# A pair's sigmoid moved behind the next step's copy, and the squares, scaling and moves of x spread over one more step each

## The chip, the cores and the metric

One core of one Trainium2 chip. The metric is device time in microseconds (us): the median of three runs of the kernel before is 1411.33 us (1408.41 to 1411.77). All times of single instructions come from one profiled execution of 1410.37 us, whose span from first to last instruction is 1408.6 us.

## The reference

Two stages. The first is attention over channels, for two matrices of 6016 x 256; the second is a gated two-layer network on 12032 rows of 256.

```
qn = q / (norm(q, axis=1) + 1e-06);  kn = k / (norm(k, axis=1) + 1e-06)
s  = kn.T @ qn / tau;  a = softmax(s, -1)          # 256 x 256
x  = (v @ a).reshape(12032, 256)
xn = x / sqrt(mean(x * x, -1) + 1e-06) * rms_g
g  = xn @ w_gate;  val = xn @ w_val                # 256 -> 1536
out = (g * sigmoid(g) * val) @ w_out               # 1536 -> 256
```

## The kernel before

The first part reads q and k and forms the score matrices (that of the second matrix beside block 0). The rows of v are worked on in 24 blocks of 512 rows (12 of each matrix, the last of each 384 rows). A block j is 12 steps f = 0 to 11, one for each 128 of the 1536 hidden columns, and in the same steps the next block's x is made ready, so that TensorE (PE) always has hidden columns to work on. Every engine takes its instructions in the order in which the code issues them; that order is written by hand, in the loop over `steps` at lines 909 to 922: the step itself, then the output products of an earlier step, then what the table `ready` lists for this f (for block j + 1), then what `extra` lists.

There are two kinds of steps. Steps 0, 1, 8 and 9 are plain (`emit_hidden`, L603): six products of 512 columns for the gate (pg), six for the value (pv). ScalarE (ACT) takes the sigmoid of pg (L624), VectorE (DVE) multiplies (L627, L634). Steps 2 to 7, 10 and 11 come in pairs (`emit_pair`, L543), two hidden blocks together by a scheme with fewer products: the even step of a pair is its gate step (k = 0), the odd one its value step (k = 1). Each has 21 products of 256 columns in four groups, each group in a PSUM bank of its own: (1,), (2, 6), (5, 7), (3, 4). ACT copies the first group out (L575, "the copy"); then DVE adds the others up in four instructions (L580 to L583). After the gate step's four sums ACT takes the sigmoid of the gate (L587), GpSimd (POOL) multiplies it by the gate (L588), and after the value step's sums POOL multiplies by the value, in two halves (L595). The halves are then rounded on ACT (L534, gh) in the next step, and DVE takes the remainder (L540, gl). The output products (L654, po) follow three steps later.

PSUM has four banks for the steps (tag "gv"). A pair step takes all four, a plain step two, in turn: the second group of a step can start when the bank of four tiles before is free, which is when L580 of the step before has read it. So a late L580 stops PE one step later, at the second group of a pair step or at pv of a plain step; a late L627 of step 9 stops PE at the third group of step 10.

The next block's x: step 0 moves v (L359), step 1 splits it (L341, L342). Steps 2 and 3 end with the products of x, one half (two tiles of 128 rows) each (`emit_x`, L377, px, 12 matmuls). ACT squares them with a running sum (L388), POOL makes the factor 1/rms (L397, L401, rr), ACT scales (L413, xn). Two transposes on DVE (L449, xw) and 16 DMAs issued one after the other by SyncE (SP, L456, xnT) turn x. In step 8 ACT scales by g (L471) and DVE forms four differences (L477, xp); steps 9 and 10 split the eight operands ("round 0" and "round 1", L487 on ACT and L489 on DVE).

In block 1 the pairs' weights are built (`build_s`, from odd steps), and in block 10 the softmax of the second matrix runs in steps 5 to 9.

Of the kernel before, what the change touches and what calls it, by code (L numbers as in the profile page):

```python
# [8 lines left out]
F32 = mybir.dt.float32  # L9
F32R = mybir.dt.float32r  # L10
U32 = mybir.dt.uint32
AF = mybir.ActivationFunctionType
# [7 lines left out]
def kernel(  # L20
# [312 lines left out]
    def half_tiles(j, h):  # L333
        return list(range(2 * h, min(2 * h + 2, blocks[j][2])))
# [33 lines left out]
    def emit_x(j, h):  # L368
        ah, al = a_hl[blocks[j][0]]
        vh, vl = vT[j]  # L370
        ts = half_tiles(j, h)
        psum, tag = (ps_s, "s") if j >= WINO and h else (ps_m, "m") if j else (ps_gv, "gv")
        px = psum.tile([P, 2, C], F32, tag=tag, name=f"px_{j}_{h}")
        for c in range(KC):
            for i, t in enumerate(ts):
                for m, (w, x) in enumerate(((vh, ah), (vl, ah), (vh, al))):
                    nc.tensor.matmul(  # L377
                        out=px[:, i, :], lhsT=w[:, c, t * P:(t + 1) * P], rhs=x[:, c, :],
                        start=(i == 0 and c == 0 and m == 0),
                        stop=(c == KC - 1 and m == 2),  # L380
                        skip_group_check=True,
                    )
        if h == 0:
            xnt[j] = xn_p.tile([P, BT, C], F32, tag="xn", name=f"xn_{j}")
        xn = xnt[j][:, 2 * h:2 * h + 2, :]
        ss = st_p.tile([P, 2], F32, tag="ss", name=f"ss_{j}_{h}")
        for i in range(len(ts)):
            nc.scalar.activation(  # L388
                out=xn[:, i, :], in_=px[:, i, :], func=AF.Square, scale=C ** -0.5,
                accum_out=ss[:, i:i + 1],  # L390
            )
        xps[j, h] = (px, ss)

    def emit_rr(j, h):
        px, ss = xps[j, h]
        nn = len(half_tiles(j, h))
        nc.gpsimd.tensor_scalar(  # L397
            out=ss[:, :nn], in0=ss[:, :nn], scalar1=1e-6, scalar2=None, op0=ALU.add
        )
        rr = st_p.tile([P, 2], F32, tag="rr", name=f"rr_{j}_{h}")  # L400
        nc.gpsimd.tensor_tensor(out=rr[:, :nn], in0=ss[:, :nn], in1=mhalf[:, :nn], op=ALU.pow)  # L401
        xps[j, h] = (px, rr)
# [140 lines left out]
    def emit_pair(j, f):  # L543
# [31 lines left out]
        nc.scalar.activation(out=zz[:, 3:4], in_=ps[0], func=AF.Copy)  # L575
        n = nt * P
        if k:
            th, zg = zs.pop((j, p))
        run_rounds()
        nc.vector.tensor_tensor(out=zz[:, 0:5:4], in0=ps[1], in1=twice(zz[:, 3:4]), op=ALU.add)  # L580
        nc.vector.tensor_tensor(out=zz[:, 1:3], in0=ps[2], in1=twice(zz[:, 4:5]), op=ALU.add)  # L581
# [1 line left out]
        nc.vector.tensor_tensor(out=zz[:, 1:3], in0=ps[3], in1=zz[:, 1:3], op=ALU.add)  # L583
        run_subs()
        if k == 0:
            th = pool["z"].tile([P, 2 * BN], F32, tag="th", name=f"th_{j}_{p}", bufs=1)
            nc.scalar.activation(out=th[:, :2 * n], in_=z[:, :2 * n], func=AF.Sigmoid)  # L587
            nc.gpsimd.tensor_tensor(out=th[:, :2 * n], in0=th[:, :2 * n], in1=z[:, :2 * n], op=ALU.mult)  # L588
            zs[j, p] = (th, z)
            return  # L590
        for i in range(2):
            hh = zg[:, i * n:(i + 1) * n]
# [86 lines left out]
    with tc.manual_schedule():  # L679
# [102 lines left out]
        decode_w(0)  # L782
        for h in range(2):
            emit_x(0, h)
        emit_rr(0, 0)
        emit_rr(0, 1)
        load_w(2)
# [88 lines left out]
            for c in range(KC):  # L876
                split_v(n, c, nc.vector if n > 1 else nc.gpsimd)

        def x_part(h):
            def go(n):  # L880
                emit_x(n, h)
                emit_rr(n, h)
            return go

        def xn_part(h):
            return lambda n: emit_xn(n, h)

        ready = {
            0: (v_moves,),
            1: (v_splits,),  # L890
            2: (x_part(0),),
            3: (x_part(1), xn_part(0)),
            4: (xn_part(1), emit_xT_move),
            8: (emit_xT_parts,),
            9: (lambda n: emit_xT_round(n, 0),),
            10: (lambda n: emit_xT_round(n, 1),),
# [1 line left out]
        ready0 = {  # L898
            1: (v_moves,),
            2: (v_splits,),  # L900
            4: (x_part(0),),
            5: (xn_part(0),),
            6: (x_part(1),),
            7: (xn_part(1),),
            8: (lambda n: emit_xT_first(n, 0),),
            9: (lambda n: emit_xT_first(n, 1),),
        }
# [52 lines left out]
```

## Time and profile before

| what | us |
|---|---|
| median of 3 runs | 1411.33 (1408.41 to 1411.77) |
| the profiled execution | 1410.37 |
| its span | 1408.6 |
| PE busy | 1332.9 (95%) |
| DVE busy | 1064.1 (76%) |
| POOL busy | 671.8 (48%) |
| ACT busy | 636.1 (45%) |

A matmul of 256 columns is shown with some 280 ns, but one starts every 0.12 us: the records overlap, so PE's share says little and its starts and idle times say more. "[0.50 <-DVE z L580]" behind a row is the engine's idle time before it and what ended it. A row of a timeline merges like instructions ("x2"), and its length is from the first's start to the last's end.

### The profile page before, as it was taken

The page shows a single profiled execution, that of the slowest core. Times are in us where ns is not written, and L with a number is a line of the kernel's source. Part 1 is how long each engine was busy: PE and PEld are TensorE (multiplying, and loading weights), DVE is VectorE, ACT ScalarE, POOL GpSimd, SP SyncE. Part 2 cuts the span into 40 slices and gives each one's busy share as a digit, 9 for nine tenths or more (in the row PEclk, how much of TensorE's full clock was granted, in tenths as well). Part 3 has the DMA queues.
Part 4 walks back from the last instruction along what each step waited for, and adds up shares of the span by engine and source line. Part 5 has one row for each costly group of instructions (what it writes and reads, how often), then busy time and mean ns, then how long its engine had stood idle before and what let it go on. Part 6 is the DMA issues. An engine that isn't in the chain of part 4 may idle for free.

```text
span 1408.6 us, 24669 instructions
## 1 busy us (share of the span) xinstructions
PE 1332.9 (95%) x9420; PEld 1243.4 (88%) x9420; DVE 1064.1 (76%) x1597; ACT 636.1 (45%) x1244; POOL 671.8 (48%) x500
## 2 busy tenths in 40 slices
PE   8877979899999999999989999999999999999998
PEld 7766868799999999999979999999999999999998
DVE  4588847787787787787776787787787787787775
ACT  4445634444444444444444444444444444444442
POOL 1045623445545455455534445455455455545544
PEclk9989989999999999999999999999999999999999
DMA  9666310101111111111102111111111111111000
GB/s 305 210 186 200 115 30 16 31 20 42 31 24 39 32 25 36 34 25 31 36 7 46 28 24 36 33 25 35 34 26 33 34 28 31 34 24 31 22 22 12
DMA packets 150871, 71.61 MB, mean 51 GB/s; under 512 B 109281, under 2 KB 136929, under 8 KB 150753
## 3 DMA queue, kind: packets, MB, share of 16 engines
q1 hardware_dynamic: 150752, 70.04, 20.0%
q8 instruction: 74, 1.21, 0.4%
q14 instruction: 45, 0.36, 0.1%
HBM read 46.40 MB, written 12.32 MB: 42 GB/s over the span
## 4 chain that ended last, share of the span: by engine, by line
PE 48%; DVE 23%; ACT 9%; issue 8%; SPq 5%; DMA 4%; POOL 2%; DVEq 0%; ACTq 0%; POOLq 0%
PE p L563 14%; PE po L654 13%; PE pv L613 6%; PE s L175 5%; SPq L456 5%; PE px L377 5%; PE pg L613 4%; DVE z L580 4%; DVE z L581 3%; DVE xt L489 3%; ACT th L587 3%; DVE z L583 3%; POOL z L595 2%; DVE z L582 2%; DMA xnT<-xw 2%
## 5 line engine op out<-in xcount | busy, mean ns | idle before, releaser
L654 PE MATMUL po<-w,gh 128*128 128x256 f32 x2256 | 410.2, 280 | 1.2 <-ACT gh L534 1.2
L654 PEld LDWEIGHTS po<-w,gh 128*128 128x128 f32 x2256 | 353.0, 189 | 10.9 <-ACT gh L534 1.8
L563 PE MATMUL p<-xt,w 128*128 128x256 f32 (+1 forms) x2112 | 315.1, 283 | 13.4 <-DVE z L580 9.2
L654 PE MATMUL po<-w,gl 128*128 128x256 f32 x1128 | 316.1, 280 | 1.8 <-DVE gl L540 1.8
L588 POOL TENSOR_TENSOR th<-th,z 128x1024 f32<-128x1024 f32 (+1 forms) x88 | 206.7, 2349 | 214.5 <-ACT th L587 214.5
L595 POOL TENSOR_TENSOR z<-th,z 128x512 f32<-128x512 f32 (+1 forms) x176 | 219.7, 1269 | 164.7 <-DVE z L583 164.7
L563 PEld LDWEIGHTS p<-xt,w 128*128 128x128 f32 x2112 | 276.9, 189 | 18.9 <-DVE z L580 13.3
L534 ACT ACTIVATE gh<-z 128x512 fp32r<-128x512 f32 (+1 forms) x264 | 163.9, 622 | 228.4 <-POOL z L595 214.1
L563 PE MATMUL p<-xt,s 128*128 128x256 f32 (+1 forms) x1584 | 217.9, 282 | 2.2 <-DVE z L582 1.1
L654 PEld LDWEIGHTS po<-w,gl 128*128 128x128 f32 x1128 | 212.7, 189 | 2.7 <-DVE gl L540 2.7
L540 POOL TENSOR_TENSOR gl<-z,gh 128x512 fp32r<-128x512 f32 (+1 forms) x88 | 120.9, 1374 | 174.5 <-ACT gh L534 173.0
L563 PEld LDWEIGHTS p<-xt,s 128*128 128x128 f32 x1584 | 199.9, 189 | 3.7 <-PE p L563 2.1
L580 DVE TENSOR_TENSOR z<-p,z 128x512 f32<-128x512 f32 (+1 forms) x176 | 118.0, 670 | 103.5 <-ACT z L575 98.9
L613 PE MATMUL pv<-xt,w 128*128 128x512 f32 (+1 forms) x672 | 175.6, 397 | 14.4 <-DVE z L580 14.4
L613 PE MATMUL pg<-xt,w 128*128 128x512 f32 (+1 forms) x672 | 177.8, 400 | 3.1 <-DVE th L627 2.0
L587 ACT ACTIVATE th<-z 128x1024 f32<-128x1024 f32 (+1 forms) x88 | 91.3, 1037 | 174.3 <-DVE z L583 174.3
L613 PEld LDWEIGHTS pv<-xt,w 128*128 128x128 f32 x672 | 125.1, 189 | 50.4 <-DVE z L580 23.3
L540 DVE TENSOR_TENSOR gl<-z,gh 128x512 fp32r<-128x512 f32 (+1 forms) x176 | 133.1, 769 | 31.2 <-ACT gh L534 24.6
L613 PEld LDWEIGHTS pg<-xt,w 128*128 128x128 f32 x672 | 120.2, 190 | 25.2 <-DVE th L627 3.2
L583 DVE TENSOR_TENSOR z<-p,z 128x512 f32<-128x512 f32 (+1 forms) x176 | 119.6, 680 | 19.4 <-DVE z L582 1.4
L581 DVE TENSOR_TENSOR z<-p,z 128x512 f32<-128x512 f32 (+1 forms) x176 | 119.6, 680 | 19.4 <-DVE z L580 1.4
L175 PE MATMUL s<-raw 128*128 128x256 f32 x376 | 93.1, 408 | 24.9 <-DMA raw<-in_k_dram 24.9
(94 smaller groups left out, 1423.3 us busy)
## 6 DMA issues: line engine op xcount, KB each, us to landing
v<-in_v_dram SPq DMA_DIRECT2D x88, 128.0 KB, 3.7
out_dram<-ob SPq DMA_DIRECT2D x88, 128.0 KB, 2.2
xnT<-xw SPq DMA_DIRECT2D x320, 32.0 KB, 1.9
raw<-in_q_dram SPq DMA_DIRECT2D x27, 256.0 KB, 4.4
raw<-in_k_dram SPq DMA_DIRECT2D x27, 256.0 KB, 4.6
raw<-in_q_dram SPq DMA_DIRECT2D x9, 512.0 KB, 5.7
raw<-in_k_dram SPq DMA_DIRECT2D x9, 512.0 KB, 6.7
wraw<-in_moe_w_gate_dram SPq DMA_DIRECT2D x12, 256.0 KB, 2.9
```

The costliest lines, as they stand in the source:

```text
L175: nc.tensor.matmul(out=s_ps[b][:, c, :], lhsT=r[:, 1, t, c * P:(c + 1) * P], rhs=r[:, 0, t, :], start=(t0 + t == 0 and c == 0), stop=(t0 + ...
L534: nc.scalar.activation(out=gh, in_=hh, func=AF.Copy)
L540: engine.tensor_tensor(out=gl, in0=hh, in1=f32(gh), op=ALU.subtract)
L563: nc.tensor.matmul(out=t[:, i, :h], lhsT=wm[wi], rhs=xm[xi], start=(i == 0 and q == 0), stop=(q == 2), skip_group_check=True,)
L580: nc.vector.tensor_tensor(out=zz[:, 0:5:4], in0=ps[1], in1=twice(zz[:, 3:4]), op=ALU.add)
L581: nc.vector.tensor_tensor(out=zz[:, 1:3], in0=ps[2], in1=twice(zz[:, 4:5]), op=ALU.add)
L583: nc.vector.tensor_tensor(out=zz[:, 1:3], in0=ps[3], in1=zz[:, 1:3], op=ALU.add)
L587: nc.scalar.activation(out=th[:, :2 * n], in_=z[:, :2 * n], func=AF.Sigmoid)
L588: nc.gpsimd.tensor_tensor(out=th[:, :2 * n], in0=th[:, :2 * n], in1=z[:, :2 * n], op=ALU.mult)
L595: nc.gpsimd.tensor_tensor(out=o, in0=i0, in1=i1, op=ALU.mult)
L613: nc.tensor.matmul(out=t[:, :n], lhsT=wgv[wi][:, f, c, wj, :], rhs=x[xi][:, c, :n], start=(m == 0), stop=(m == 3 * KC - 1),)
L654: nc.tensor.matmul(out=o_ps[j][t // 2][:, t % 2, :], lhsT=g[:, t * P:(t + 1) * P], rhs=wo[w][:, f, :], start=(f == 0 and t % 2 == 0 and m ...
```

## The change

The sigmoid of a pair's gate and POOL's product with the gate are issued in the value step, behind that step's copy, and no longer at the end of the gate step. The squares of each half of x, with the factor behind them, are issued one step after the products of x; the scaling of each half one step later than before; and the transposes with the 16 moves in step 5 in place of step 4. For block 0 (`ready0`) the order stays. No instruction is added or left out.

```diff
@@ emit_x @@
+        xps[j, h] = px
+
+    def emit_x_squares(j, h):
+        px = xps[j, h]
+        ts = half_tiles(j, h)
         if h == 0:
             xnt[j] = xn_p.tile([P, BT, C], F32, tag="xn", name=f"xn_{j}")
...
@@ emit_pair @@
         nc.scalar.activation(out=zz[:, 3:4], in_=ps[0], func=AF.Copy)
         n = nt * P
         if k:
-            th, zg = zs.pop((j, p))
+            zg = zs.pop((j, p))
+            th = pool["z"].tile([P, 2 * BN], F32, tag="th", name=f"th_{j}_{p}", bufs=1)
+            nc.scalar.activation(out=th[:, :2 * n], in_=zg[:, :2 * n], func=AF.Sigmoid)
+            nc.gpsimd.tensor_tensor(out=th[:, :2 * n], in0=th[:, :2 * n], in1=zg[:, :2 * n], op=ALU.mult)
         run_rounds()
...
         run_subs()
         if k == 0:
-            th = pool["z"].tile([P, 2 * BN], F32, tag="th", name=f"th_{j}_{p}", bufs=1)
-            nc.scalar.activation(out=th[:, :2 * n], in_=z[:, :2 * n], func=AF.Sigmoid)
-            nc.gpsimd.tensor_tensor(out=th[:, :2 * n], in0=th[:, :2 * n], in1=z[:, :2 * n], op=ALU.mult)
-            zs[j, p] = (th, z)
+            zs[j, p] = z
             return
...
@@ the loop over steps @@
+        def x(h):
+            return lambda n: emit_x(n, h)
+
+        def squares_of_x(h):
+            return lambda n: (emit_x_squares(n, h), emit_rr(n, h))
+
+        def xn(h):
             return lambda n: emit_xn(n, h)
 
         ready = {
             0: (v_moves,),
             1: (v_splits,),
-            2: (x_part(0),),
-            3: (x_part(1), xn_part(0)),
-            4: (xn_part(1), emit_xT_move),
+            2: (x(0),),
+            3: (squares_of_x(0), x(1)),
+            4: (xn(0), squares_of_x(1)),
+            5: (xn(1), emit_xT_move),
             8: (emit_xT_parts,),
```

In the rows of the programs below, z0_9_p is the gate tile and z1_9_p the value tile of pair p in block 9 (p = 1, 2, 3, 5 are steps 2 and 3, 4 and 5, 6 and 7, 10 and 11), th its sigmoid; names with _10_ belong to the x of block 10, which is made in block 9. Line numbers of the changed program run 5 to 8 higher here.

ACT in steps 2 to 5 of block 9, before: from the sigmoid of step 2 to the copy of step 5.

```order
L587 ACTIVATE th_9_1_6476<-z0_9_1_6468 128x1024
L668 ACTIVATE ob_8_6491<-po1_8_5921 128x512
L388 ACTIVATE xn_10_6511,ss_10_0_6512<-px_10_0_6498 128x256 x2
L575 ACTIVATE z1_9_1_6543<-p1_9_3_6518 128x256
L388 ACTIVATE xn_10_6511,ss_10_1_6582<-px_10_1_6569 128x256 x2
L413 ACTIVATE xn_10_6511<-px_10_0_6498,rr_10_0_6516 128x256 x2
L575 ACTIVATE z0_9_2_6615<-p1_9_4_6590 128x256
L534 ACTIVATE gh_9_2_6551<-z0_9_1_6468 128x512
L534 ACTIVATE gh_9_3_6553<-z0_9_1_6468 128x512
L587 ACTIVATE th_9_2_6625<-z0_9_2_6615 128x1024
L413 ACTIVATE xn_10_6511<-px_10_1_6569,rr_10_1_6586 128x256 x2
L575 ACTIVATE z1_9_2_6687<-p1_9_5_6662 128x256
```

The same stretch in the changed program, from the output's copy in step 2 to the scaling of the second half of x.

```order
L673 ACTIVATE ob_8_6488<-po1_8_5914 128x512
L580 ACTIVATE z1_9_1_6533<-p1_9_3_6508 128x256
L585 ACTIVATE th_9_1_6535<-z0_9_1_6468 128x1024
L393 ACTIVATE xn_10_6562,ss_10_0_6563<-px_10_0_6495 128x256 x2
L580 ACTIVATE z0_9_2_6607<-p1_9_4_6582 128x256
L539 ACTIVATE gh_9_2_6544<-z0_9_1_6468 128x512
L539 ACTIVATE gh_9_3_6546<-z0_9_1_6468 128x512
L418 ACTIVATE xn_10_6562<-px_10_0_6495,rr_10_0_6567 128x256 x2
L393 ACTIVATE xn_10_6562,ss_10_1_6631<-px_10_1_6569 128x256 x2
L580 ACTIVATE z1_9_2_6662<-p1_9_5_6637 128x256
L585 ACTIVATE th_9_2_6664<-z0_9_2_6607 128x1024
L418 ACTIVATE xn_10_6562<-px_10_1_6569,rr_10_1_6635 128x256 x2
```

The sigmoid stands behind the copy of steps 3 and 5, each set of squares behind the copy of the step that follows its products, and the scaling of the second half in step 5.

ACT in steps 10 to 0, before: round 1 (xt0 from xp) and what stands around it.

```order
L575 ACTIVATE z0_9_5_6918<-p1_9_10_6893 128x256
L534 ACTIVATE gh_9_9_6874<-z1_9_4_6869 128x512
L587 ACTIVATE th_9_5_6926<-z0_9_5_6918 128x1024
L487 ACTIVATE xt0_10_6846<-xp_10_6848 128x512 x2
L575 ACTIVATE z1_9_5_6970<-p1_9_11_6945 128x256
L624 ACTIVATE z0_10_0_7008<-pg_10_0_6994 128x512
```

The same in the changed program.

```order
L580 ACTIVATE z0_9_5_6918<-p1_9_10_6893 128x256
L539 ACTIVATE gh_9_9_6874<-z1_9_4_6869 128x512
L492 ACTIVATE xt0_10_6846<-xp_10_6848 128x512 x2
L580 ACTIVATE z1_9_5_6967<-p1_9_11_6942 128x256
L585 ACTIVATE th_9_5_6969<-z0_9_5_6918 128x1024
L629 ACTIVATE z0_10_0_7008<-pg_10_0_6994 128x512
```

Round 1 comes ahead of the sigmoid and no longer behind it.

DVE from the last sum of step 4 to the first of step 6, before.

```order
L583 TENSOR_TENSOR z0_9_2_6615<-p3_9_4_6608,z0_9_2_6615 128x512
L540 TENSOR_TENSOR gl_9_2_6552<-z0_9_1_6468,gh_9_2_6551 128x512
L540 TENSOR_TENSOR gl_9_3_6554<-z0_9_1_6468,gh_9_3_6553 128x512
L449 STREAM_TRANSPOSE xw_10_6642<-xn_10_6511 128x4x4x32 x2
L580 TENSOR_TENSOR z1_9_2_6687<-p2_9_5_6666,z1_9_2_6687 128x2x256
L581 TENSOR_TENSOR z1_9_2_6687<-p5_9_5_6673,z1_9_2_6687 128x512
L582 TENSOR_TENSOR z1_9_2_6687<-p5_9_5_6673,z1_9_2_6687 128x256
L583 TENSOR_TENSOR z1_9_2_6687<-p3_9_5_6680,z1_9_2_6687 128x512
L580 TENSOR_TENSOR z0_9_3_6736<-p2_9_6_6715,z0_9_3_6736 128x2x256
```

The same in the changed program.

```order
L591 TENSOR_TENSOR z0_9_2_6607<-p3_9_4_6600,z0_9_2_6607 128x512
L545 TENSOR_TENSOR gl_9_2_6545<-z0_9_1_6468,gh_9_2_6544 128x512
L545 TENSOR_TENSOR gl_9_3_6547<-z0_9_1_6468,gh_9_3_6546 128x512
L588 TENSOR_TENSOR z1_9_2_6662<-p2_9_5_6641,z1_9_2_6662 128x2x256
L589 TENSOR_TENSOR z1_9_2_6662<-p5_9_5_6648,z1_9_2_6662 128x512
L590 TENSOR_TENSOR z1_9_2_6662<-p5_9_5_6648,z1_9_2_6662 128x256
L591 TENSOR_TENSOR z1_9_2_6662<-p3_9_5_6655,z1_9_2_6662 128x512
L454 STREAM_TRANSPOSE xw_10_6691<-xn_10_6562 128x4x4x32 x2
L588 TENSOR_TENSOR z0_9_3_6736<-p2_9_6_6715,z0_9_3_6736 128x2x256
```

The two transposes of x (xw_10) stand behind the sums of step 5, no longer ahead of them.

## Rows read from the trace of the kernel before

**Rows 1.** The page: the busy time of each engine over the whole span.

```profile
PE 1332.9 (95%) x9420; PEld 1243.4 (88%) x9420; DVE 1064.1 (76%) x1597; ACT 636.1 (45%) x1244; POOL 671.8 (48%) x500
```

**Rows 2.** Busy time in one whole block (block 9, from the first product of its step 0 to that of the next block's). Columns: stretch, its length, busy time of PE, PEld, DVE, ACT, POOL with counts, granted clock, DMA share, GB/s.

```profile
620.17:672.48 52.31, 51.41 (x387) 48.67 (x385) 40.92 (x64) 23.88 (x49) 27.19 (x21) 1.00 0.13 29
```

**Rows 3.** Who PE waited for from 260 us on. Columns: total us, times, the longest.

```profile
PE pv L613 <- DVE z L580: 14.4, 21, 1.6
...
PE p L563 <- DVE z L580: 9.2, 20, 1.4
...
PE p L563 <- DVE z L627: 2.4, 3, 1.5
```

**Rows 4.** Timeline of PE in block 9: start, length, instruction. Steps 0, 1, 2, 3, 4 start at 620.17, 625.14, 629.35, 634.68, 640.02; step 6 at 647.82 (its second group at 648.73), step 7 at 652.38.

```profile
620.17 1.56 PE L613 MATMUL pg<-xt,w 128*128 128x512 f32 x6
...
622.23 1.67 PE L613 MATMUL pv<-xt,w 128*128 128x512 f32 x6 [0.50 <-DVE z L580]
...
625.14 1.57 PE L613 MATMUL pg<-xt,w 128*128 128x512 f32 x6
...
629.35 0.88 PE L563 MATMUL p<-xt,w 128*128 128x256 f32 x6
...
634.68 0.88 PE L563 MATMUL p<-xt,w 128*128 128x256 f32 x6
...
640.02 0.88 PE L563 MATMUL p<-xt,w 128*128 128x256 f32 x6
...
647.82 0.52 PE L563 MATMUL p<-xt,w 128*128 128x256 f32 x3
...
648.73 0.62 PE L563 MATMUL p<-xt,w 128*128 128x256 f32 x3 [0.40 <-DVE z L580]
...
652.38 0.88 PE L563 MATMUL p<-xt,w 128*128 128x256 f32 x6
```

**Rows 5.** Timeline of ACT in block 9: squares, copies, a scaling, a sigmoid and round 1 in steps 3 to 6 and 10.

```profile
640.22 0.39 ACT L388 ACTIVATE xn<-px 128x256 f32<-128x256 f32 x1 [2.83 <-PE px L377]
...
641.65 0.40 ACT L575 ACTIVATE z<-p 128x256 f32<-128x256 f32 x1
...
645.95 0.82 ACT L413 ACTIVATE xn<-px,rr 128x256 f32<-128x256 f32 x2
...
648.37 0.38 ACT L575 ACTIVATE z<-p 128x256 f32<-128x256 f32 x1 [1.33 <-PE p L563]
...
669.13 1.06 ACT L587 ACTIVATE th<-z 128x1024 f32<-128x1024 f32 x1 [2.99 <-DVE z L583]
...
670.09 1.14 ACT L487 ACTIVATE xt<-xp 128x512 fp32r<-128x512 f32 x2
```

**Rows 6.** Timeline of DVE in the same block: the sums of step 4, the transposes, the first sum of step 5; then round 0, the last sum of step 10, round 1, the first sum of step 11.

```profile
642.15 0.69 DVE L580 TENSOR_TENSOR z<-p,z 128x512 f32<-128x512 f32 x1 [1.99 <-ACT z L575]
...
644.20 0.69 DVE L583 TENSOR_TENSOR z<-p,z 128x512 f32<-128x512 f32 x1
...
646.80 1.30 DVE L449 STREAM_TRANSPOSE xw<-xn 128x512 f32<-128x512 f32 x2 [0.71 <-ACT xn L413]
...
648.03 0.65 DVE L580 TENSOR_TENSOR z<-p,z 128x512 f32<-128x512 f32 x1
...
665.10 1.29 DVE L489 TENSOR_TENSOR xt<-xnT,xt 128x512 fp32r<-128x512 f32 x2
...
668.35 0.69 DVE L583 TENSOR_TENSOR z<-p,z 128x512 f32<-128x512 f32 x1
...
670.74 3.14 DVE L489 TENSOR_TENSOR xt<-xp,xt 128x512 fp32r<-128x512 f32 x2 [1.71 <-ACT xt L487]
...
673.81 0.68 DVE L580 TENSOR_TENSOR z<-p,z 128x512 f32<-128x512 f32 x1
```

**Rows 7.** Timeline of POOL in the same block: both products of step 3, the factor of the second half of x, the gate's product of step 10.

```profile
640.24 2.55 POOL L595 TENSOR_TENSOR z<-th,z 128x512 f32<-128x512 f32 x2 [0.70 <-DVE z L583]
...
642.87 0.22 POOL L397 TENSOR_SCALAR ss<-ss 128x2 f32<-128x2 f32 x1
...
643.17 0.71 POOL L401 TENSOR_TENSOR rr<-ss,mhalf 128x2 f32<-128x2 f32 x1
...
670.33 2.40 POOL L588 TENSOR_TENSOR th<-th,z 128x1024 f32<-128x1024 f32 x1 [2.80 <-ACT th L587]
```

**Rows 8.** Timeline of SP: the 16 moves of x in block 9, in block 12 (among the shortest), in block 20 (the longest from block 2 on) and in block 11 (384 rows).

```profile
648.17 10.71 SPq L456 DMA_DIRECT2D xnT<-xw  x16
...
807.97 10.18 SPq L456 DMA_DIRECT2D xnT<-xw  x16
...
1229.07 11.32 SPq L456 DMA_DIRECT2D xnT<-xw  x16
...
758.94 11.20 SPq L456 DMA_DIRECT2D xnT<-xw  x16
```

**Rows 9.** Timeline of ACT: the first instruction on the moved x, in blocks 9 and 11; of DVE: the first product of step 9 in block 9; of PE: the third group of step 10 in block 11.

```profile
661.34 1.32 ACT L471 ACTIVATE xnT<-xnT,g_sb 128x512 f32<-128x512 f32 x2
...
771.51 1.34 ACT L471 ACTIVATE xnT<-xnT,g_sb 128x512 f32<-128x512 f32 x2 [1.54 <-DMA xnT<-xw]
...
663.71 0.68 DVE L627 TENSOR_TENSOR z<-z,pg 128x512 f32<-128x512 f32 x1
...
774.50 0.91 PE L563 MATMUL p<-xt,s 128*128 128x192 f32 x6 [0.31 <-DVE z L627]
```

More of the change, by code (lines that the diff above doesn't have):

```diff
@@ L784 @@
             emit_x(0, h)
+            emit_x_squares(0, h)
         emit_rr(0, 0)
@@ L877, in v_splits @@
                 split_v(n, c, nc.vector if n > 1 else nc.gpsimd)
[L879 to L885, printed above, removed]
+        def x(h):
[3 more added lines that the diff above has]
+        def xn(h):
             return lambda n: emit_xn(n, h)
@@ L900 @@
             2: (v_splits,),
[L901 to L904, printed above, removed]
+            4: (x(0), squares_of_x(0)),
+            5: (xn(0),),
+            6: (x(1), squares_of_x(1)),
+            7: (xn(1),),
             8: (lambda n: emit_xT_first(n, 0),),
```

## Prediction

> **What bounds the kernel now.** I read the page's busy times first: PE 95%, no other engine over 76% [rows 1]. That alone doesn't make PE the bound, so the second view is one whole block in the stretches: 52.31 us, PE busy in 51.41 of them at a granted clock of 1.00, DVE in 40.92 [rows 2]. What is left to gain is time in which PE stands still, and the third view, whom PE waited for from 260 us on, names it: 14.4 us before pv and 9.2 us before a pair's products, both for DVE's first sum L580, in 21 and 20 blocks [rows 3]. So each block stalls twice, once in each way.
>
> The fourth view is PE's timeline of block 9, for what such a stall really costs. Step 0 takes 625.14 - 620.17 = 4.97 us, step 1, as much work, 4.21. Step 6 takes 652.38 - 647.82 = 4.56, while steps 4 and 5 together take 647.82 - 640.02 = 7.80, 3.90 each [rows 4]. The stalls cost 0.76 and 0.66 us and are shown as 0.50 and 0.40: some 0.26 each is hidden in the tail of the last matmul and in the restart. Over the kernel that is 14.4 + 21 x 0.26 = 19.9 and 9.2 + 20 x 0.26 = 14.4, together 34.3 us. This is what the change can get.
>
> **Why L580 is late.** For pv it is the first sum of step 11, which starts at 673.81 because round 1 on DVE stands before it: it began only at 670.74, 1.70 after the last sum of step 10 had ended (668.35 + 0.69), and took 3.14 where the same pair in round 0 took 1.29 [rows 6]. It began late because ACT's part of round 1 (670.09) stands behind the sigmoid, which waited 2.99 for that last sum [rows 5]. It was slow because POOL's gate product ran from 670.33 to 672.73 [rows 7]: both round 1 instructions ended behind it. For step 6 it is the first sum of step 5 (648.03), behind the transposes, which waited for ACT's scaling (645.95) [rows 5, 6]; that stands behind the sigmoid of step 4.
>
> The Trainium skill, "SBUF — State Buffer", section "SBUF: two separate sides", says that a DVE instruction with two SBUF inputs and a GpSimd instruction that reads SBUF exclude each other for a whole instruction, whichever starts first. The 3.14 against 1.29 agrees with it. The rule also speaks against a piece of this change; see the first rival.
>
> **The change, part by part.** No instruction is added, so the cost is one of order and waits. I follow block 9 with PE unhindered from step 2 on (3.90 for a pair step, 4.20 for a plain one, 5.33 with products of x [rows 4]): step 3 starts at 634.68, 4 at 640.02, 5 at 643.92, 6 at 647.82, 7 at 651.72, 8 at 655.62, 9 at 659.82, 10 at 664.03, 11 at 667.93, the next step 0 at 671.83 with pv at 673.23. A copy can start 0.55 after its step (647.82 to 648.37 [rows 4, 5]); the first sum some 1.3 after it, an estimate from nine matmuls at 0.12 and the tail of the last; the four sums take 644.20 + 0.69 - 642.15 = 2.74 [rows 6].
>
> Squares a step later. In step 3 ACT waited 2.83 for the products of x with the copy of step 4 queued behind the squares, so that copy came at 641.65 [rows 5], 1.6 after its step began, and the sums at 642.15. Now the copy comes at 640.57 and the sums run from 641.3 to 644.0, the two remainders to 645.3.
>
> The sigmoid behind the copy. Step 3: copy from 635.23, sigmoid 635.6 to 636.7 (1.06 at 669.13 [rows 5]), gate product to 639.1 (2.40), value products to 641.7 (2.55 [rows 7]). They started at 640.24 before, so gh comes no later although POOL's work begins later. What is queued behind: on ACT the squares (0.8, with room up to the next copy); on POOL the factor of the first half of x, which used to run between the two products and now runs behind them, 641.7 to 642.7 (1.01 from 642.87 to 643.17 + 0.71 [rows 7]).
>
> The chain of x from there: scaling of the first half to 643.6 (0.82), squares of the second to 644.4, its factor to 645.5, then behind the copy and sigmoid of step 5 (end 645.9) the scaling of the second half, to 646.7. The transposes stand behind the sums of step 5, which run from 645.3 to 648.1: the chain of x has 1.4 us to spare. Transposes 648.1 to 649.4 (1.30). The first sum of step 5 is done at 646.0, PE wants its bank at 648.2: the stall of step 6 goes. Step 6's first sum starts at 649.4, done at 650.1; step 7 wants that bank at 652.1.
>
> The moves. SP starts them at 649.5 instead of 648.17, 1.3 later, and needs 10.2 to 11.3 us to issue them (10.71 in block 9, 10.18 in block 12, 11.32 the longest [rows 8]). In block 11, the one place where ACT waited for them, L471 started 771.51 - (758.94 + 11.20) = 1.37 after the last issue [rows 8, 9]. So L471 starts between 661.0 and 662.1, about 661.5; before it started at 661.34, held by ACT's own rounding [rows 9]. From L471 on DVE is one rigid chain: the first product of step 9 (L627) ends 663.71 + 0.68 - 661.34 = 3.05 later [rows 9], and it frees the bank of step 10's third group, wanted nine matmuls after that step's start, at 664.03 + 9 x 0.12 = 665.1. The limit for L471 is therefore 662.05, and only the slowest moves pass it. I charge 0.1 us a block, 2 us in all; the ends are 0 and 1 (first rival).
>
> Round 1. ACT does its part behind the copy of step 10, so DVE starts it at once after the last sum of step 10, which ends 668.35 + 0.69 - 661.34 = 7.70 after L471: at 669.2. The sigmoid waits for the same sum, so POOL's gate product starts 1.06 plus handing over later, at 670.4; the second half of round 1 starts at 669.8, ahead of it. So 1.29 and not 3.14, and the first sum of step 11 is done at 671.2, 2 us before pv wants it. The stall of step 0 goes, and 2 us of lateness more would not bring it back.
>
> Outside the regular blocks: in block 1 the transposes now share step 5 with a weight build, in block 10 with the second matrix's norms, both on DVE. No row shows that; the ends are 0 and the transposes' own 1.30 in each. I take 2 together, near the upper end, since DVE is what PE waits for there.
>
> The sum: -34.3 + 2 + 2 = -30.3. The profiled execution took 1410.37 us (span 1408.6 and 1.8 around it), so 1380.1 for one like it; it lies 1.0 under the median of the runs shown, hence 1381 for a median.
>
> **Rivals.**
>
> The moves land late. For: the slack of L471 is 0.5 us, and the factor of the second half (POOL, 644.5 to 645.5) now runs beside DVE's remainders (644.0 to 645.3), which no stretch of the trace before shows together. By the rule of the Trainium skill named above, a remainder would wait out POOL's factor. As a mechanism of this kernel: a remainder stands behind the factor (up to 1.0 us) as round 1 stood behind the gate product, so the sums of step 5, the transposes and L471 shift by 0.5 to 1.0, L471 comes at 662.0 to 662.5, with slow moves at 663.1, and each block gives back 0 to 1.0. PE has stopped at this very place (2.4 us for L627 [rows 3], 0.31 in block 11 right behind the wait for the moves [rows 9]). With 0.5 a block: 20 x 0.5 = 10 us, 1391; at worst 1402. Chance 0.20.
>
> Only one stall goes: POOL's gate product gets in ahead of the second half of round 1, which then ends 2.4 us later, and pv's stall stays. Against it: 0.6 us between the two starts. Then only the 14.4 of step 6 are gained, with the same 4 charged: 1411.3 - 14.4 + 4 = 1401. Chance 0.06.
>
> Slower: the chain of x through ACT and POOL, now with gate and value products ahead of the first factor, ends late. It must cost more than the 1.42 gained a block: L471 behind 663.5, moves beginning behind 651.5, the last scaling behind 650.2 instead of 646.7. That point is 3.5 us off; every us beyond it costs 20. With POOL held up a step (3.90), 0.4 beyond: 1419. Chance 0.07.
>
> No difference: gain and late moves cancel, or the waits only change their names. Chance 0.05.
>
> **The numbers.** Forecast 0.62, its own range 1374 to 1388 (no charge at all and a few us of PE's smaller waits; 0.4 us a block). With the rivals the range is 1373 to 1402. About 0.3% (4.2 us) is what a measurement can tell from no change: faster 0.88, within 0.05, slower 0.07.
>
> **What would show it.** A block of about 51.0 us; no wait of pv or of step 6 for the first sum; the copy of step 4 some 0.6 us after its step; round 1 in 1.3 us, starting where the last sum of step 10 ends; the transposes behind the sums of step 5. L471 should wait for DMAs in most blocks, for 1 to 2.5 us, with no PE stop at the third group of step 10. It is wrong if PE stops there by 0.4 us or more in most blocks, if the transposes start after 650 (on this clock), or if round 1 still takes 3 us.

## The result and the profile after

The changed kernel took 1377.82 us (median of 4 runs, 1377.68 to 1378.17), the kernel before, run beside it, 1411.31 (4 runs). The ratio is 0.9767, 95% interval 0.975 to 0.9784: some 33 us less. The forecast was 1381, range 1373 to 1402.

The page of the changed kernel, its span and its busy times, beside [rows 1]:

```profile
span 1375.9 us, 24750 instructions
...
PE 1322.1 (96%) x9420; PEld 1244.3 (90%) x9420; DVE 1013.4 (74%) x1597; ACT 645.9 (47%) x1244; POOL 677.2 (49%) x500
```

The counts are the same: only order and waits changed. DVE is 51 us less busy although it does the same work: some 39 of it (21 blocks x 1.86) because round 1 no longer stands still inside its instructions, as shown below, 15 in the remainders (the group of L540 had 133.1 us, that of L545 has 117.8). Whom PE waited for from 260 us on (total us, times, the longest), beside [rows 3]:

```profile
PE p L568 <- DVE z L632: 6.3, 3, 2.6
PE po L659 <- DVE gl L545: 1.4, 2, 1.1
PE po L659 <- ACT gh L539: 0.7, 1, 0.7
```

Both lines that named the first sum (14.4 and 9.2 us, then L580, now L588) are gone. The one that grew, for L632, is 2.4 before. Of its 6.3 us, 2.58 is a wait in block 2 that was there before too, at 258 us, just outside that view; 1.48 stands in block 10 as before (1.49); 2.28 stands in block 11, where it was 0.31 [rows 9], and comes back below.

Busy time of block 9 in the columns of [rows 2]:

```profile
613.12:664.30 51.18, 51.18 (x386) 48.77 (x385) 38.53 (x64) 24.38 (x49) 27.50 (x21) 1.00 0.14 29
```

51.18 us instead of 52.31, and PE is shown without an idle moment. The first products of its steps 0, 1, 6, 7, 10 and 11 (start, length, instruction):

```profile
613.12 1.56 PE L618 MATMUL pg<-xt,w 128*128 128x512 f32 x6
...
617.31 1.57 PE L618 MATMUL pg<-xt,w 128*128 128x512 f32 x6
...
639.98 0.88 PE L568 MATMUL p<-xt,w 128*128 128x256 f32 x6
...
643.88 0.88 PE L568 MATMUL p<-xt,w 128*128 128x256 f32 x6
...
656.19 0.88 PE L568 MATMUL p<-xt,w 128*128 128x256 f32 x6
...
660.40 0.88 PE L568 MATMUL p<-xt,w 128*128 128x256 f32 x6
```

Step 0 lasts 617.31 - 613.12 = 4.19 (4.97 before), step 6 643.88 - 639.98 = 3.90 (4.56 before). Step 10 lasts 660.40 - 656.19 = 4.21 instead of 3.90: a loss of 0.31 that the view of waits doesn't show at all.

The same reading for blocks 2 to 22 of both traces, the lengths of each step added up (before minus after), says where the time went:

| steps | us less than before | of it |
|---|---|---|
| 0 | 19.62 | pv's stall |
| 6 | 14.62 | the stall of step 6 |
| 10 | -3.53 | -1.55 in the blocks of 512 rows, -1.98 in block 11 |
| 1 and 2 | 2.06 | 0.71 in block 2's step 2 (runs of one and the same kernel differ more there) |
| 9 and 11 | 2.03 | 1.71 in block 10 |
| 3 to 5, 7, 8 | -0.35 | |

That is 34.45, and block 23 adds 1.01. Up to block 2 the changed kernel is 2.84 behind (249.60 against 246.76), which leaves 32.6 of the spans' 32.7 (1408.6 - 1375.9). Of that 2.84, block 1 lost 1.69 (it takes 58.87 instead of 57.18), in its steps 7 to 9, where PE waits 0.37 and 1.08 for products that stand behind weight builds on DVE. The sigmoid's part alone, below, takes as long in these three steps as the kernel before, so the loss is the table's. The other 1.15 had been lost when block 1 began (190.73 against 189.58), within what the loads at the start vary by: two runs of one and the same kernel below began it at 191.79 and 190.03.

Now the mechanism. ACT in block 9: the copies of steps 4 and 5 with the sigmoid and the scaling behind, the first instruction on the moved x, round 1, the sigmoid of step 11 (in brackets the idle time before and whose end closed it):

```profile
632.79 0.39 ACT L580 ACTIVATE z<-p 128x256 f32<-128x256 f32 x1 [3.33 <-PE p L568]
...
636.92 1.05 ACT L585 ACTIVATE th<-z 128x1024 f32<-128x1024 f32 x1
638.06 0.84 ACT L418 ACTIVATE xn<-px,rr 128x256 f32<-128x256 f32 x2
...
654.28 1.34 ACT L476 ACTIVATE xnT<-xnT,g_sb 128x512 f32<-128x512 f32 x2 [2.68 <-DMA xnT<-xw]
...
658.71 1.14 ACT L492 ACTIVATE xt<-xp 128x512 fp32r<-128x512 f32 x2
...
662.09 1.06 ACT L585 ACTIVATE th<-z 128x1024 f32<-128x1024 f32 x1 [0.74 <-DVE z L591]
```

DVE in the same block: the first sum of step 4, the remainders, the first sum of step 5, the transposes, the last sum of step 10, round 1, the first sum of step 11:

```profile
633.51 0.69 DVE L588 TENSOR_TENSOR z<-p,z 128x512 f32<-128x512 f32 x1 [2.59 <-PE p L568]
...
636.17 1.28 DVE L545 TENSOR_TENSOR gl<-z,gh 128x512 fp32r<-128x512 f32 x2
637.41 0.69 DVE L588 TENSOR_TENSOR z<-p,z 128x512 f32<-128x512 f32 x1
...
640.07 1.30 DVE L454 STREAM_TRANSPOSE xw<-xn 128x512 f32<-128x512 f32 x2
...
661.30 0.69 DVE L591 TENSOR_TENSOR z<-p,z 128x512 f32<-128x512 f32 x1
661.91 1.28 DVE L494 TENSOR_TENSOR xt<-xp,xt 128x512 fp32r<-128x512 f32 x2
663.11 0.68 DVE L588 TENSOR_TENSOR z<-p,z 128x512 f32<-128x512 f32 x1
```

Round 1 follows the last sum at once and takes 1.28, where it waited 1.71 and took 3.14 in [rows 6]. POOL's gate product of step 11 waits for the sigmoid (662.09 + 1.06 = 663.15) and starts at 663.29, when round 1 is just over (661.91 + 1.28 = 663.19); the factor of the second half of x is the line above it:

```profile
637.01 1.02 POOL L406 TENSOR_TENSOR rr<-ss,mhalf 128x2 f32<-128x2 f32 x1
...
663.29 2.42 POOL L586 TENSOR_TENSOR th<-th,z 128x1024 f32<-128x1024 f32 x1 [2.79 <-ACT th L585]
```

SP's 16 moves of x in the same block, beside [rows 8]:

```profile
641.43 11.48 SPq L461 DMA_DIRECT2D xnT<-xw  x16
```

They begin 641.43 - 621.51 = 19.92 after step 2 starts (18.82 before), and L476 waits for the last of them: 641.43 + 11.48 + 1.37 = 654.28.

### The profile page after: what moved, and what is told of

The parts are those of the page before. It is cut to its first block, busy times and chain, and to the rows that moved or that the text cites. A ratio compares the mean times of both kernels' runs of the same rounds, so it can differ in the third digit from the quotient of the medians.

```text
span 1375.9 us, 24750 instructions
## 1 busy us (share of the span) xinstructions
PE 1322.1 (96%) x9420; PEld 1244.3 (90%) x9420; DVE 1013.4 (74%) x1597; ACT 645.9 (47%) x1244; POOL 677.2 (49%) x500
## 4 chain that ended last, share of the span: by engine, by line
PE 85%; DVE 7%; DMA 2%; ACT 2%; issue 1%; SPq 1%; POOL 0%; DVEq 0%; ACTq 0%; POOLq 0%
PE p L568 31%; PE po L659 26%; PE pg L618 9%; PE pv L618 9%; PE s L175 5%; PE px L377 5%; DMA raw<-in_k_dram 2%; DVE acc L197 1%; DVE wx L120 1%; DVE hh L639 1%; SPq L461 1%; DVE wk L521 1%; DVE th L632 0%; ACT sq L188 0%; DMA raw<-in_q_dram 0%
## 5 line engine op out<-in xcount | busy, mean ns | idle before, releaser
L568 PE MATMUL p<-xt,w 128*128 128x256 f32 (+1 forms) x2112 | 311.2, 282 | 4.8 <-DVE z L632 4.1
L545 POOL TENSOR_TENSOR gl<-z,gh 128x512 fp32r<-128x512 f32 (+1 forms) x88 | 119.3, 1355 | 240.8 <-ACT gh L539 230.1
L588 DVE TENSOR_TENSOR z<-p,z 128x512 f32<-128x512 f32 (+1 forms) x176 | 119.4, 678 | 105.2 <-PE p L568 102.0
L580 ACT ACTIVATE z<-p 128x256 f32<-128x256 f32 (+1 forms) x176 | 66.7, 379 | 201.2 <-PE p L568 197.2
L629 ACT ACTIVATE z<-pg 128x512 f32<-128x512 f32 (+1 forms) x88 | 51.4, 584 | 161.9 <-PE pg L618 161.3
L545 DVE TENSOR_TENSOR gl<-z,gh 128x512 fp32r<-128x512 f32 (+1 forms) x176 | 117.8, 702 | 5.9 <-ACT gh L539 5.0
```

The source lines that it names most:

```text
L545: engine.tensor_tensor(out=gl, in0=hh, in1=f32(gh), op=ALU.subtract)
L568: nc.tensor.matmul(out=t[:, i, :h], lhsT=wm[wi], rhs=xm[xi], start=(i == 0 and q == 0), stop=(q == 2), skip_group_check=True,)
```

## The experiments

The question behind them: the change has two parts, the sigmoid with its gate product in the value step, and the table (squares, scaling and moves of x a step later). One theory: the stalls share one cause, the sigmoid's place at the end of the gate step. It holds round 1 back until POOL's gate product runs beside it, and in step 4 it holds the second scaling and with it the transposes back; moving it alone removes both stalls, and the table only costs. The rival: each part removes a stall of its own, the sigmoid pv's, the table step 6's, because only it puts the transposes behind the sums of step 5.

**The sigmoid's part alone.** From the changed kernel, the table set back:

```diff
         ready = {
-            2: (x(0),),
-            3: (squares_of_x(0), x(1)),
-            4: (xn(0), squares_of_x(1)),
-            5: (xn(1), emit_xT_move),
+            2: (x(0), squares_of_x(0)),
+            3: (x(1), squares_of_x(1), xn(0)),
+            4: (xn(1), emit_xT_move),
```

> The sigmoid and the gate product moved as in the change, the table for x as before (squares in the step of their products, transposes and moves in step 4). Theory 1 (the sigmoid's place is behind both stalls): round 1 takes 1.3 us and pv's stall (20 us) goes; the scaling no longer waits for the sigmoid, so the transposes of step 4 start right behind the remainders and the first sum of step 5 ends about 0.1 us before PE wants it: step 6 loses 0 to 0.3 us a block; with the moves earlier again there is no cost of late moves: 1375 to 1383. Rival (the two parts of the change each remove one stall, the table that of step 6): only pv's 20 us, 1390 to 1393.

Measured: 1374.88 us (1373.7 to 1375.67, 4 runs; before 1411.2), ratio 0.9743, interval 0.9729 to 0.9758. A regular block takes 50.90, step 0 4.21, step 6 3.93, step 10 3.90. DVE in block 9 (step 6 begins at 639.79): remainders, transposes, the first sum of step 5, and round 1.

```profile
636.78 1.28 DVE L545 TENSOR_TENSOR gl<-z,gh 128x512 fp32r<-128x512 f32 x2
637.98 1.30 DVE L454 STREAM_TRANSPOSE xw<-xn 128x512 f32<-128x512 f32 x2
639.20 0.65 DVE L588 TENSOR_TENSOR z<-p,z 128x512 f32<-128x512 f32 x1
...
660.01 1.28 DVE L494 TENSOR_TENSOR xt<-xp,xt 128x512 fp32r<-128x512 f32 x2
```

The transposes still stand ahead of the first sum, as in [rows 6], but they follow the remainders without the 0.71 us of waiting. That is all the stall of step 6 needed. The first theory stands and its rival falls: the sigmoid's part alone removes both stalls. The moves start at 639.34, 2 us earlier than in the changed kernel (block 9 begins at 612.91 here and at 613.12 there), and ACT doesn't wait for them at all:

```profile
652.24 1.32 ACT L476 ACTIVATE xnT<-xnT,g_sb 128x512 f32<-128x512 f32 x2
```

Even the copy of step 4, which still stands behind the second squares and starts 1.6 us after its step, costs PE nothing that shows: steps 4 and 5 take 3.90 as before, step 6 is within 0.03 of that.

Which PSUM bank a group of products gets is not the same in all these programs. As built, the sigmoid's part alone has the same banks as the kernel before in every step of blocks 2 to 9, and the changed kernel has others. Both lose both stalls, so the banks don't explain the gain there.

**The table alone.** From the changed kernel, the sigmoid and its product set back into the gate step:

```diff
         if k:
-            zg = zs.pop((j, p))
-            th = pool["z"].tile([P, 2 * BN], F32, tag="th", name=f"th_{j}_{p}", bufs=1)
-            nc.scalar.activation(out=th[:, :2 * n], in_=zg[:, :2 * n], func=AF.Sigmoid)
-            nc.gpsimd.tensor_tensor(out=th[:, :2 * n], in0=th[:, :2 * n], in1=zg[:, :2 * n], op=ALU.mult)
+            th, zg = zs.pop((j, p))
...
         if k == 0:
-            zs[j, p] = z
+            th = pool["z"].tile([P, 2 * BN], F32, tag="th", name=f"th_{j}_{p}", bufs=1)
+            nc.scalar.activation(out=th[:, :2 * n], in_=z[:, :2 * n], func=AF.Sigmoid)
+            nc.gpsimd.tensor_tensor(out=th[:, :2 * n], in0=th[:, :2 * n], in1=z[:, :2 * n], op=ALU.mult)
+            zs[j, p] = (th, z)
```

> The table of the change, with sigmoid and gate product at the end of the gate step as before. Theory: step 6's stall (14 us) goes, pv's stays at 0.5 to 0.9 us shown a block, round 1 still 3.1 us; some 4 us for late moves as in the changed kernel: 1398 to 1402. Rival (squares a step later are what frees DVE everywhere, and an earlier DVE also starts round 1 early enough): pv's stall goes too, 1380 to 1385.

Measured: 1452.27 (1451.81 to 1454.18, 4 runs), ratio 1.0295, interval 1.028 to 1.031. The expectation had the wrong sign. Whom PE waited for from 260 us on (the first sum is L585 in this program, the sigmoid L592):

```profile
PE pv L618 <- DVE z L585: 26.7, 20, 1.6
PE p L568 <- ACT z L580: 17.8, 18, 1.0
PE p L568 <- DVE z L632: 11.5, 11, 4.1
```

The stall of step 6 has changed its cause. ACT from the sigmoid of step 4 on:

```profile
660.84 1.06 ACT L592 ACTIVATE th<-z 128x1024 f32<-128x1024 f32 x1 [1.39 <-DVE z L588]
661.80 0.82 ACT L418 ACTIVATE xn<-px,rr 128x256 f32<-128x256 f32 x2
...
665.52 0.84 ACT L418 ACTIVATE xn<-px,rr 128x256 f32<-128x256 f32 x2 [1.89 <-POOL rr L406]
666.25 0.38 ACT L580 ACTIVATE z<-p 128x256 f32<-128x256 f32 x1
```

Behind the late sigmoid come the first scaling, the second squares and the copy of step 5. The second scaling waits 1.89 for POOL's factor, and the copy of step 6 is queued behind it; step 6's third group of products waits 0.99 for that copy (5.16 us for the step instead of 3.90).

pv's stall has grown, from 14.4 to 26.7 us, and this I had not foreseen. L476 starts at 680.09, held by late moves. With the sigmoid in the gate step, DVE's way from there is rigid as far as pv: the first sum of step 11 starts at 692.57, 12.48 after L476.

```profile
680.09 1.34 ACT L476 ACTIVATE xnT<-xnT,g_sb 128x512 f32<-128x512 f32 x2 [2.21 <-DMA xnT<-xw]
...
692.57 0.68 DVE L585 TENSOR_TENSOR z<-p,z 128x512 f32<-128x512 f32 x1
```

In the kernel before, it was 673.81 - 661.34 = 12.47 [rows 6, 9]. So what L476 is late against PE arrives at pv undiminished, up to the point where the same chain stops PE already in step 10: from there on step 10 takes up the rest (3.95 to 5.19 in the regular blocks), and step 0 stays at 5.87 to 5.90. In the changed kernel the same way takes 663.11 - 654.28 = 8.83.

**Only the moves a step later.** To part the two causes: the kernel before, sigmoid as there, squares in the step of their products as there (in the change's helpers), and of the table only the scaling of the second half, the transposes and the moves in step 5.

```diff
         ready = {
-            2: (x_part(0),),
-            3: (x_part(1), xn_part(0)),
-            4: (xn_part(1), emit_xT_move),
+            2: (x(0), squares_of_x(0)),
+            3: (x(1), squares_of_x(1), xn(0)),
+            5: (xn(1), emit_xT_move),
```

> The kernel before with only the scaling of the second half, the transposes and the moves of x in step 5 instead of 4: squares in the step of their products, sigmoid and gate product at the end of the gate step. Theory A (the table alone was slow for two reasons: copy 5 queued behind sigmoid, scaling and squares on ACT, and late moves, whose lateness the slow round 1 hands on to pv in full): with the squares back, step 6 loses nothing (3.9), but L476 still comes some 1 to 2 us late, so that steps 10 and 11 lose 0.3 to 0.6 and step 0 1.6 to 1.9 a block: 1420 to 1432. Theory B (the sixth step itself, not the squares, made PE wait in step 6): step 6 still takes 5.1, 1445 to 1455. Rival to both (late moves are hidden): 1395 to 1400.

Measured: 1437.74 (1435.32 to 1440.71, 4 runs; before 1411.11), ratio 1.019, interval 1.0174 to 1.0206. Step 6 takes 3.90 in the regular blocks, as expected, since the transposes stand behind the sums of step 5. Step 0 takes 5.87 to 5.90 there (4.9 to 5.4 before), step 10 4.36 to 5.35, more than expected, hence a time above the range.

```profile
PE pv L618 <- DVE z L585: 26.6, 20, 1.6
PE p L568 <- DVE z L632: 17.7, 19, 3.5
```

So the growth of pv's stall from 14.4 to 26.6 us comes from the late moves alone. L476 at 673.20 and the first sum of step 11 at 685.68 are again 12.48 apart.

```profile
673.20 1.34 ACT L476 ACTIVATE xnT<-xnT,g_sb 128x512 f32<-128x512 f32 x2 [2.08 <-DMA xnT<-xw]
...
685.68 0.68 DVE L585 TENSOR_TENSOR z<-p,z 128x512 f32<-128x512 f32 x1
```

The wait for the copy of step 6 in the run before this one is gone. With the earlier squares that copy starts 0.55 after its step (659.01 against 658.46) and not 1.78 (666.25 against 664.47). But the banks differ too: in the table alone the third group of step 6 takes the bank that this copy frees, here one that DVE frees in step 5. This run doesn't part the two.

What the moves a step later give at step 6 (0.66 a block) they take back more than twice over at pv and in step 10.

**Round 1 as late as before, but with POOL kept out.** From the kernel before, to see whether the late start of round 1 or the gate product beside it makes pv's stall. The gate product of the last pair goes into the value step, behind a small copy of one column of round 1's result, so that POOL can't start it sooner (the copied value is not used):

```diff
         if k:
             th, zg = zs.pop((j, p))
+            if p == 5:
+                if j + 1 < NB:
+                    seen = st_p.tile([P, 1], F32, tag="seen", name=f"seen_{j}")
+                    nc.gpsimd.tensor_copy(seen, f32(xp[j + 1][1][:, 7, 0:1]))
+                nc.gpsimd.tensor_tensor(out=th[:, :2 * n], in0=th[:, :2 * n], in1=zg[:, :2 * n], op=ALU.mult)
...
-            nc.gpsimd.tensor_tensor(out=th[:, :2 * n], in0=th[:, :2 * n], in1=z[:, :2 * n], op=ALU.mult)
+            if p != 5:
+                nc.gpsimd.tensor_tensor(out=th[:, :2 * n], in0=th[:, :2 * n], in1=z[:, :2 * n], op=ALU.mult)
```

> The kernel before, where POOL's gate product of the last pair alone (step 10) first copies one column of round 1's result, so that it can't start before round 1 has ended; sigmoid and table as before. Theory (round 1 is slow because it shares SBUF with POOL's product, and its slowness makes the stall, not its late start): round 1 starts as late as before but takes 1.3 us and not 3.1, pv's stall goes, step 6's stays: 1390 to 1393. Rival (the late start behind the sigmoid is enough for the stall): 1405 to 1412.

Measured: 1391.84 (1389.78 to 1394.02, 4 runs), ratio 0.9859, interval 0.9842 to 0.9877. Round 1 on DVE:

```profile
667.74 1.29 DVE L489 TENSOR_TENSOR xt<-xp,xt 128x512 fp32r<-128x512 f32 x2 [1.71 <-ACT xt L487]
```

POOL's product starts right behind it:

```profile
669.24 2.40 POOL L583 TENSOR_TENSOR th<-th,z 128x1024 f32<-128x1024 f32 x1
```

Round 1 waits 1.71, as in [rows 6], but takes 1.29 and not 3.14. Step 0 takes 4.22, step 6 still 4.56. So the late start costs pv nothing; the time that POOL's product holds DVE does. This is the exclusion that the prediction took from the Trainium skill ("SBUF — State Buffer", section "SBUF: two separate sides"), now with the product moved and nothing else but the small copy on POOL ahead of it. The 1.29 against 3.14 agrees with it.

**Moves in step 4, with the sigmoid moved.** From the changed kernel:

```diff
-            4: (xn(0), squares_of_x(1)),
-            5: (xn(1), emit_xT_move),
+            4: (xn(0), squares_of_x(1), xn(1), emit_xT_move),
```

> The changed kernel with the scaling of the second half, the transposes and the moves of x back in step 4, behind the squares of the second half. Theory (squares a step later are what forces the moves into the sixth step: POOL's factor comes too late for step 4): the scaling waits for the factor until some 6 us after step 4's start, DVE stands still for it, the first sum of step 5 ends 0.6 us after PE wants its bank, step 6 loses 0.6 to 0.9 us a block, against 4 us less for late moves: 1387 to 1392. Rival (the step of the moves doesn't matter as long as the sigmoid is out of the way): 1374 to 1378.

Measured: 1400.77 (1399.46 to 1401.29, 4 runs), ratio 0.9926, interval 0.9912 to 0.9939, above both ranges. Step 10 is back at 3.90 and step 0 stays at 4.20, but step 6 takes 5.14. Whom PE waited for:

```profile
PE p L568 <- DVE z L590: 9.1, 23, 0.7
PE p L568 <- DVE z L588: 7.2, 19, 0.5
```

The transposes wait 1.48 for the second scaling, which waits 1.47 for the factor, since the squares come a step late here. The stall for L588 was expected. The second one in the same step, for the third sum L590, was not, and doubles the price. In this program and in the changed one the third group of step 6 takes the PSUM bank that DVE's third sum of step 5 frees; in the kernel before it takes the one that ACT's copy frees. The built programs show the same: of the tiles of steps 4 to 6 in block 9, the third group of step 6 has the bank of step 5's third group here and in the changed kernel, and in the kernel before that of step 6's own first group. My picture of the banks as handed out strictly in turn was too simple.

**Moves in step 6.** From the changed kernel, to put a price on moves that are late by a whole step:

```diff
-            5: (xn(1), emit_xT_move),
+            5: (xn(1),),
+            6: (emit_xT_move,),
```

> The changed kernel with the transposes and the moves of x one step later still (step 6 instead of 5). Theory (L476 has no more than 0.5 us of reserve before DVE's chain behind it stops PE at the third group of step 10): L476 comes some 4 us later and every block loses 3.5 to 4.0 us in step 10: 1446 to 1460. Rival (there is a reserve of some us, or PE's loss is made good elsewhere): under 1410.

Measured: 1523.0 (1522.75 to 1523.24, 2 runs), ratio 1.0794, interval 1.0772 to 1.0816. The place is as expected: step 10 takes 10.1 to 11.4, and the wait for L632 is 99.7 us in 23 waits. The price is double. PE in step 10 of block 8, and the granted clock there (stretch, its length, busy times, clock, DMA share, GB/s):

```profile
653.85 1.44 PE L568 MATMUL p<-xt,s 128*128 128x256 f32 x5 [5.11 <-DVE z L632]
```

```profile
647.50:653.80 6.30, 1.23 (x11) 1.03 (x9) 2.12 (x5) 3.07 (x6) 0.66 (x1) 0.81 0.09 22
653.80:656.00 2.20, 2.15 (x10) 2.15 (x11) 2.10 (x4) 1.96 (x5) 1.30 (x2) 0.50 0.00 0
656.00:658.00 2.00, 2.00 (x11) 2.00 (x11) 1.76 (x4) 0.29 (x1) 0.93 (x1) 0.50 0.00 0
658.00:660.00 2.00, 2.00 (x18) 2.00 (x17) 1.64 (x3) 0.68 (x2) 0.00 (x0) 0.93 0.00 0
```

The stop is 5.11 us, longer than I had worked out, and behind it the clock stands at 0.50 (1.2 of 2.4 GHz) for over 4 us. Step 10 lost 11.25 - 3.90 = 7.35 there: 5.11 + 0.26 for the stop, some 2 for the slow products after it.

**Both once more, on one chip.** The changed kernel and the sigmoid's part alone, unchanged, to see whether the few us between them hold:

> The changed kernel once more, beside the next one, for a direct comparison on one chip: 1377 to 1379 by every theory.

> The sigmoid and the gate product moved alone, once more. Theory (the table costs what late moves cost: 1.6 us in the regular blocks, some 2 in block 11, some 1.5 in block 1, less 0.6 for step 6): 3 to 5 us faster than the changed kernel, 1373 to 1375. Rival (the first difference came from the chips): the same as the changed kernel within 1 us.

Measured: 1377.9 (1376.57 to 1380.42, 5 runs), ratio 0.9763, interval 0.975 to 0.9776; and 1374.22 (1371.43 to 1377.68, 4 runs), ratio 0.974, interval 0.9723 to 0.9757. The medians are 3.7 us apart, 2.9 in the first comparison; the intervals overlap by a little, so the time alone doesn't settle it. The traces do for its cause: from block 2 to 22 step 10 takes 3.48 us less in all without the table, step 6 1.39 more (4.12 and 1.38 in the second pair), and steps 7 to 9 of block 1 take 1.69 less (1.67). The sigmoid's part alone is the fastest version that ran, by its median.

## Why the prediction was right, and where it wasn't

The result came as forecast, and in the changed kernel so did the mechanism. The walk through block 9 holds step by step (before's clock minus 7.84, the difference of the starts of step 2, 629.35 and 621.51):

| | predicted | measured |
|---|---|---|
| copy of step 4 | 632.73 | 632.79 |
| first sum of step 4 | 633.5 | 633.51 |
| second scaling ends | 638.9 | 638.90 |
| transposes | 640.3 | 640.07 |
| moves begin | 641.7 | 641.43 |
| L476 | 653.2 to 654.3 | 654.28 |
| round 1 | 661.4 | 661.91 |
| first sum of step 11 done | 663.4 | 663.79 |

The two stalls. Predicted gain 19.9 and 14.4; the step lengths gave 19.62 and 14.62. The 0.26 added to each shown wait was needed: the waits alone are 14.4 and 9.2. That the second comes out so well is in part luck: of the 9.2, one wait of 1.41 stands in step 11 of block 10 and not in step 6, while step 6 of block 11 gave 1.61, where only one wait of 0.57 had been counted.

The moves. Predicted cost 2, measured 3.53. The 0.1 a block was about right in the regular blocks (1.55 in all): seven of them lost 0.16 to 0.31 in step 10, where L476 came at or just past the limit that the walk gave (654.28 against 662.05 - 7.84 = 654.21 in block 9). The sum missed block 11. Its own 384 rows make a pair step 3.40 and not 3.90, but the moves in it are of block 12's x with 512 rows (the "384 rows" of [rows 8] are the block's own) and take SP as long (10.78). So with a step later they cost it more: L476 waited 3.96 and PE's stop grew.

```profile
757.96 1.33 ACT L476 ACTIVATE xnT<-xnT,g_sb 128x512 f32<-128x512 f32 x2 [3.96 <-DMA xnT<-xw]
```

```profile
760.94 0.91 PE L568 MATMUL p<-xt,s 128*128 128x192 f32 x6 [2.28 <-DVE z L632]
```

Step 10 there takes 5.93, against 3.95 before and 4.01 with the sigmoid's part alone. Block 11 was the one place that [rows 9] showed already stopped behind its moves, so the row was there and the term was not worked out for it. The second run of the changed kernel lost more there: step 10 of block 11 takes 6.95, of 3.97 lost in all step 10s.

Blocks 1 and 10. Charged 2 together. Block 1 lost 1.69, more than its half. Block 10 got shorter beyond its two stalls, by 1.71 in its steps 9 and 11; the sigmoid's part alone shows nearly the same (2.91 for the whole block against 3.00), so it belongs to that part. The 1.11 in step 11 come from the banks, which the prediction didn't have: before, the second group of that step took the bank that DVE's first sum of step 10 frees, behind the softmax, and PE waited 1.41 for it; in the changed kernel and in the sigmoid's part alone it has the bank of the step's own first group, and PE waits 0.47 for ACT's copy, though DVE's order there is the same. Which instruction gives the 0.60 in step 9 I did not follow. So the late moves were 1.5 and block 1 0.7 too cheap, and block 10 was wrong by 2.7, with the other sign; outside these terms 3.0 us of small gains (the rest of the table above and block 23) stand against 1.15 lost at the start. Such errors partly cancel, and it is luck that the sum is nearer to the result, 30.3 against 32.7 for the profiled executions, than its smaller terms are to theirs.

The rivals. That POOL's factor would meet DVE's remainders was right: it ran from 637.01, they from 636.17 to 637.45. But DVE was first, so POOL paid, 1.02 for the factor instead of 0.71 [rows 7], and DVE lost nothing. The rule works both ways, and the rival had it in one direction. Round 1 stayed ahead of the gate product, as forecast: the product waited for its sigmoid and started 0.10 after round 1 had ended. The long chain of x ended where predicted, at 638.9, over 1 us ahead of the transposes.

What the prediction didn't see is that half of the change gains nothing. It named the sigmoid as the cause of both stalls and then took the way past step 6's through the whole table. Had it asked what the sigmoid's move alone does to the transposes, the walk would have shown them free with their place unchanged.

## What to carry to other kernels

When a wait ends late, follow it to the instruction that is late for everyone, and work out what moving that one alone does before more is moved: here one of two parts carried all the gain, and the other, alone, makes the kernel 27 us slower even in its milder form. A transfer issued later has to be checked in the shortest block, whose steps shrink while the issue time of its moves doesn't. And where one engine's instructions form a rigid chain between a transfer and PE, lateness at its head arrives undiminished, as long as PE isn't stopped nearer to the head; loosening the chain (12.5 to 8.8 us here) can be worth more than the transfer's start.

## What the runs showed of the hardware that was not expected

A stop of PE can cost more than itself. After the 5.11 us in the run with the moves in step 6 the granted clock was 0.50 for over 4 us, and the block lost some 2 us more than the stop. The trace of the changed kernel shows the same once, behind the stop of 2.58 us in block 2, which follows another of 1.54 seven us earlier (the kernel before has both stops and 0.50 behind them too); behind that of 2.28 us in block 11 the clock stayed at 1.00. Both stretches, in the columns of [rows 2]:

```profile
261.25:264.00 2.75, 2.61 (x10) 2.24 (x11) 2.59 (x5) 1.96 (x5) 1.21 (x1) 0.50 0.00 0
...
760.90:763.00 2.10, 2.06 (x18) 2.06 (x19) 2.01 (x4) 1.86 (x5) 1.20 (x2) 1.00 0.00 0
```

In the second run of the same kernel the stop in block 11 was 2.67 us, and within 2 us of its end the granted clock was at 0.50; steps 10 and 11 of that block took 1.92 us more together than in the first run. So a charge for a stop of some us has to leave room for slow products behind it. The short stalls of before left the clock at 1.00 [rows 2].

POOL pays for DVE as DVE does for POOL: a factor of 128 x 2 numbers took 1.02 us where a DVE remainder ran over its start, and 0.71 elsewhere. The Trainium skill, "SBUF — State Buffer", section "SBUF: two separate sides", says that whichever starts first has the port for its whole instruction. The trace agrees: the factor ended 0.58 after the remainder.

SP needed 10.2 to 11.6 us for the 16 moves in both kernels [rows 8], whatever the rows in them (in the changed kernel 10.93 for the 384 rows moved in block 10, 10.78 and 11.48 for 512 in blocks 11 and 9), and in the changed kernel their reader started 1.37 to 1.38 after SP had issued the last, where it waited for them.
